# Starting addresses of matmul operands, and the order of a few queue steps, in a clustered-attention kernel with two dense layers

## The chip, the cores and the metric

The kernel runs on 1 core of one Trainium2 chip. The metric is device time in microseconds (us), the median of several executions. Before the change it is 785.4 us (three runs, 784.46 to 785.62).

The engines are named as the profile names them: PE (TensorE, with PEld for its weight loads), DVE (VectorE), ACT (ScalarE), POOL (GpSimd) and SP (SyncE, which here only issues DMAs). "SPq" in a row is the time that SP needs to issue a DMA.

## What is computed

Attention in which a query sees only the keys of its own cluster, and then two dense layers (`moe`, `moe2`) on the 1536 rows that it leaves. B = 2, H = 8, S = 768, D = 64, 16 clusters, 512 columns, 2048 hidden columns, all float32.

```python
q_assign = argmax(normalize(q) @ normalize(centroids).T)      # k_assign likewise
scores = where(q_assign[:, None] == k_assign[None, :], q @ k.T / sqrt(D), -1e9)
x = softmax(scores) @ v                      # -> (B*S, H*D) = (1536, 512)
h = x @ moe_w_in;    x = (h * cos(h)) @ moe_w_out
h = x @ moe2_w_in
g = where(h >= 1, h, where(h <= -1, 0, (h + 1)**2 / 4))
out = g @ moe2_w_out
```

## The kernel before

**Order.** Every engine takes its instructions in the order in which the code issues them (`manual_schedule`). So a step written ahead of another one runs ahead of it on each engine that both use, SP's DMA queue included.

**Attention.** Two heads make a pair; there are 8 pairs (`pairs`). `prep_pair(i)` is a generator of 12 steps, one per `yield`: steps 1 to 4 turn q and k (`ptq`, L492) and split them into a high and a low part `th`, `tl` on POOL (L474, L475); step 5 multiplies with the centroids (`dt`, L513) and moves the result out (`dc`, ACT L516); step 6 turns it back (`pd`, L520); steps 7 to 11 find the cluster as a one-hot row (DVE L529, L530, POOL L532, DVE L537, L539), with `stack_head(0)` in step 9; step 12 turns the one-hots (`po`, `oht`) and calls `one_hots(0)`. `stack_head(h)` is five DMAs from SP that copy `th` and `tl` into the score operands `st` of one head; `one_hots(h)` is four more, from `oht`. Those of head 0 are issued inside the steps. Those of head 1 are appended to the list `second` as one function, `second_head`, and run later. `th` and `tl` have one buffer each; pairs 1, 3 and 5 use a spare slot (`w_1`) in their place, so only pairs 6 and 7 follow one another in the same buffer.

`run_cycle(d, order)` runs one head (d = 0 to 15) from a string of words: S a block of scores (`scores_of`: PE L580 and L583, then DVE L589), E its exponential on ACT (L598), T and t a transpose of p on PE (L635) with its copy out by ACT or DVE (L638), V the product with v (`p_v`, 24 matmuls, L649), R the row sums turned into factors (DVE L605 to L608, POOL L611, a DMA `flat`), B two DMAs that spread the factors (`rb`, L622), X the scaling on DVE (L654), Y the split into `xh`, `xl` on POOL (five instructions, L664 to L669), P the next step of `prep_pair`, K the oldest entry of `second`, W one step of a weight conversion. Even heads use `EVEN`, odd ones `ODD`; d = 0, 13, 14 and 15 have strings of their own. `first_pair()` prepares pair 0 and is written out by hand.

**Dense layers.** `hidden` and `output` are pure matmul streams of 512 columns, fp32r, three matmuls (L785 to L787, `mm3`) for each product. A block is 48 matmuls (four output tiles of 12); there are 24 blocks of `h` and 24 of `y`, 2304 matmuls in all, one stream on PE. In `h` the stationary operand is a weight slot and the moving one `xh` or `xl`. In `y` of the first layer the stationary operand is a weight slot and the moving one `gh` or `gl`; in the second layer these two change places. The weights go round four slots `w_0` to `w_3`: of the eight quarters (l, qi), `h` takes slot 0 where qi is even and slot 2 where it is odd, `y` slot 1 where qi is even and slot 3 where it is odd.

**Layout.** Tiles lie in SBUF one behind the other in the order of the code, each partition's bytes padded to 32. 16384 bytes of scratch and 128 bytes of constants come first. Then `cpool`: ident 512, desc 64, ohscale 32, ohbias 32, own 32, row 96, ones 128, cn32 512, xh 24576, xl 24576. Then `w0pool`: wraw 8192, w_1 16384, wx 4096, w_0 16384. Then `xpool`: rec 128, den 3 x 128, turned 128, line 512, rb 2 x 1536. Then, during attention, `apool` (pt 12 x 1536, nat 6144, css 128, th, tl 6144 each, six st of 6144, dots, oht, four t32 and eq of 1536 each, three v32 of 3072, two mx of 128, eight nm of 32, six p of 3072), and after it, from the same start, `mpool` (w_2, w_3 16384 each, acc 3 x 8192, gh 2 x 8192, gl 2 x 8192 and tiles of 2048).

Lines that the prediction speaks of:

```python
nat[1] = [...]                                                                   # L261
nc.scalar.activation(nat[1][0][...], y.to_broadcast([P, 2]), AF.Exp, scale=0.0)  # L262: loads Exp's table
nc.vector.tensor_scalar(y, y, 1e-30, None, ALU.max)                              # L265: writes y
```

Of the kernel before, what the change touches and what calls it, by code (L numbers as in the profile page):

```python
# [9 lines left out]
F32 = mybir.dt.float32  # L10
# [4 lines left out]
AF = mybir.ActivationFunctionType  # L15
# [4 lines left out]
P = 128  # L20
# [13 lines left out]
def attention_moe_moe(  # L34
# [19 lines left out]
    B, H, S, D = q.shape  # L54
# [20 lines left out]
    cpool = ctx.enter_context(tc.tile_pool(name="cpool", bufs=1))  # L75
    ident = cpool.tile([P, P], F32, name="ident")
    desc = cpool.tile([P, C], F32, name="desc")
# [1 line left out]
    ohbias = cpool.tile([P, 1], F32, name="ohbias")  # L79
    own = cpool.tile([P, 2, 2], F32, name="own")  # L80
    row = cpool.tile([P, 24], I32, name="row")[:, 0:1]
    ones = cpool.tile([P, 32], F32, name="ones")
    mone, half = ones[:, 0:1], ones[:, 1:2]
    cn32 = cpool.tile([P, NPAIR, 2, C], F32, name="cn32")
    nc.gpsimd.iota(row, pattern=[[0, 1]], base=0, channel_multiplier=1)
# [48 lines left out]
    xpool = ctx.enter_context(tc.tile_pool(name="xpool", bufs=1))  # L134
# [70 lines left out]
    with ExitStack() as actx:  # L205
        ap = actx.enter_context(tc.tile_pool(name="apool", bufs=1))
# [47 lines left out]
        def centroid_setup(ct):  # L254
            sq = ct[:, 1]
            nc.vector.tensor_tensor(sq, ct[:, 0], ct[:, 0], ALU.mult)
            ss = ap.tile([P, 32], F32, tag="css", name="css")
            nc.vector.tensor_reduce(ss[:, 0:1], sq, AX.X, ALU.add)
            y = ss[:, 1:2]
            sq = nc.scalar.activation(y, ss[:, 0:1], AF.Sqrt)  # L260
            nat[1] = [w0pool.tile([P, 2, NJ, 2, D], F32, tag="wraw", bufs=1, name="nat1")]  # L261
            nc.scalar.activation(nat[1][0][:, :, 0, 0, 0:1].rearrange("p s o -> p (s o)"),  # L262
                                 y.to_broadcast([P, 2]), AF.Exp, scale=0.0)
            for _ in range(2):
                nc.vector.tensor_scalar(y, y, 1e-30, None, ALU.max)  # L265
                nc.vector.reciprocal(ss[:, 2:3], y)
                nc.vector.scalar_tensor_tensor(
                    ss[:, 3:4], ss[:, 0:1], ss[:, 2:3], y, ALU.mult, ALU.add)
                nc.vector.tensor_scalar(y, ss[:, 3:4], 0.5, None, ALU.mult)
            nc.vector.tensor_scalar(ss[:, 2:3], y, 1e-6, None, ALU.add)  # L270
            nc.vector.reciprocal(ss[:, 3:4], ss[:, 2:3])
            cd = ap.tile([P, HS], F32, tag="pt", bufs=PT_BUFS, name="cd")[:, :P].rearrange(
                "p (r d) -> p r d", r=2)
            for r in range(2):
                done = nc.vector.tensor_scalar(cd[:, r], ct[:, 0], ss[:, 3:4], None, ALU.mult)
            return cd, done

        prepped = {}
        second = []

        def first_pair():
# [35 lines left out]
            def turn(s, hf):  # L317
                qk[s, hf] = bank(f"qk0_{s}_{hf}")
                for jj in range(HJ):
                    nc.tensor.transpose(qk[s, hf][:, jj * P:(jj + 1) * P],  # L320
                                        t[:, s, hf * HJ + jj].rearrange("p h d -> p (h d)"), ident)
# [7 lines left out]
            pc = ps_t.tile([P, HS], F32, tag="t", name="pc")[:, :P]  # L329
            turn(0, 0)  # L330
            turn(0, 1)
            nc.tensor.transpose(pc, cd.rearrange("p r d -> p (r d)"), ident)
            turn(1, 0)
            turn(1, 1)
            run_idle(NIDLE[1])
            pcv = pc.rearrange("p (g h c) -> p g h c", h=2, c=C)
# [3 lines left out]
            for s, hf in ((0, 0), (0, 1), (1, 0)):  # L340
                nc.scalar.activation(t32[s][hf], qk[s, hf], AF.Copy,
                                     scale=D ** -0.5 if s == 0 else 1.0)
# [99 lines left out]
            ps_q.close()  # L442
            ps_s.append(actx.enter_context(tc.tile_pool(name="ps_s", bufs=2, space=PSUM)))
            scores_of(0)
            scores_of(1)
            row_exp(0)
            po = [turn_rows(1, s) for s in range(2)]
            put_rows(1, 0, po[0], nc.scalar)
# [3 lines left out]
        def prep_pair(i):  # L452
# [4 lines left out]
            if i in (1, 3, 5):  # L457
                t2 = w0pool.tile([P, 2, 2, S], F32R, tag="w_1", name=f"t2_{i}")
# [18 lines left out]
            def stack_head(h):  # L477
                rows = slice(h * D, (h + 1) * D)
                t = st[h][0]
                copy(t[0:D], th[rows, 0].unsqueeze(1).to_broadcast([D, 2, S]))  # L480
                copy(t[D:P, 0], tl[rows, 0])
                t = st[h][1]
                copy(t[0:D, 0], th[rows, 1])
                copy(t[D:P, 0], th[rows, 1])
                copy(t[0:D, 1], tl[rows, 1])
# [47 lines left out]
                eq, eq, desc.unsqueeze(1).to_broadcast([P, G, C]), ALU.mult)  # L533
            yield
            stack_head(0)
            yield
            nc.vector.tensor_reduce(mx, eq, AX.X, ALU.max)  # L537
            yield
# [12 lines left out]
            def one_hots(h):  # L551
                for s in range(2):
                    for par in range(2):
                        r0 = par * 64 + s * 32 + h * C
                        dst = st[h][s][D:D + C, 1].rearrange(
                            "c (par jp n) -> c par jp n", par=2, n=P)[:, par]
                        copy(dst, oht[r0:r0 + C])

            def second_head():
                stack_head(1)  # L560
                one_hots(1)

            one_hots(0)
            second.append(second_head)
            yield

        units = [(i, h, hf) for i in range(len(pairs)) for h in range(2) for hf in range(2)]
# [16 lines left out]
                             start=False, stop=True)  # L584

        def row_max(n):
            nm = ap.tile([P, 1], F32, tag="nm", bufs=8, name=f"nm{n}")
            s = ptile[n]
            nc.vector.tensor_reduce(nm, s[:, :, :HS], AX.XY, ALU.max, negate=True)  # L589
            ptile[n] = (s, nm)  # L590

        def row_exp(n):
            s, nm = ptile[n]
            d, jj = divmod(n, NJ)
            if jj == 0:
                dens[d] = xpool.tile([P, 32], F32, tag="den", bufs=3, name=f"den{d}")
            p = ap.tile([P, 2, HS], F32, tag="p", bufs=P_BUFS, name=f"p{n}")
            nc.scalar.activation(p, s[:, :, :HS], AF.Exp, bias=nm,  # L598
                                 accum_out=dens[d][:, jj:jj + 1])
            ptile[n] = p  # L600
# [23 lines left out]
        dens = {}  # L624
# [47 lines left out]


        NDBL = len(units) // 2
        rec = xpool.tile([P, 32], F32, tag="rec", name="rec")
        nc.gpsimd.memset(rec, 0.0)
        made = chain.from_iterable(prep_pair(i) for i in range(1, len(pairs)))

# [2 lines left out]
        def scores_of(n):  # L681
            scores(n, 0)
            scores(n, 1)
            row_max(n)

        def run_cycle(d, order):


            for word in order.split():
                what, arg = word[0], int(word[1:] or 0)  # L690
                n = NJ * d + arg
                if what == "S":
                    if n < NJ * NDBL:
                        scores_of(n)
                elif what == "E":
                    if n < NJ * NDBL:
                        row_exp(n)
                elif what in "Tt":
                    p_transpose(2 * d + arg // NJ, arg % NJ, what == "t")
                    next_slot()  # L700
                elif what == "P":
                    next(made, None)
                elif what == "R":
                    inverse(d)
                elif what == "V":
                    p_v(d)
                elif what == "X":
                    if opsum:
                        x_rows(min(opsum))
                elif what == "K":  # L710
                    if second:
                        second.pop(0)()
                elif what == "B":
                    spread()
                elif what == "Y":
                    if x32s:
                        x_parts()
                elif what in "Ww":
                    pump(1 if d >= FIRST + (what == "w") else 0)
                elif what == "N":  # L720
                    next_slot()
            if d == 3:
                issue_chunk(0)

        PRE = "P S8 P E8"
        BEGIN = "S3 P T0 T1 S4 E3 P T2 E4 P T3 S5 E5 t4 T5 S6 T6 T7 E6 P R S7 t8 T9 E7 T10 P S8 P E8 B P S9 P t11 S10 V E9 E10"
        EVEN = "P S5 T0 T1 P t2 E5 S6 T3 P T4 E6 t5 S7 R T6 P T7 E7 S8 X T8 T9 E8 Y t10 B S9 P w P E9 t11 S10 W E10 V"
        ODD = "K S5 T0 T1 P t2 S6 E5 T3 X T4 t5 S7 Y E6 P T6 R E7 T7 S8 P E8 t8 T9 S9 T10 B P t11 E9 W S10 V P P E10 W"
        LATE_ODD = "S5 T0 T1 t2 E5 S6 T3 K R T4 t5 S7 X Y E6 T6 T7 E7 S8 E8 t8 T9 S9 T10 B t11 S10 E9 V W W W E10"
        LATE_EVEN = "S5 T0 t1 t2 E5 S6 T3 T4 E6 R T5 S7 X Y E7 T6 S8 T7 t8 W S9 E8 t9 B T10 E9 t11 W S10 V E10 W"  # L730
        LAST = "S5 T0 E5 t1 T2 T3 X t4 R t5 Y t6 T7 t8 B T9 t10 T11 W V W W W X Y"
        first_pair()
        for d in range(-1, NDBL):
            run_cycle(d, PRE if d < 0 else BEGIN if d == 0 else
                      {13: LATE_ODD, 14: LATE_EVEN, 15: LAST}.get(d, (EVEN, ODD)[d % 2]))
        manual.close()
# [138 lines left out]
```

## Time and profile before

| | us |
|---|---|
| median of the runs shown | 785.4 (784.46, 785.40, 785.62) |
| the profiled execution, its own time | 787.31 |
| its span, first to last instruction | 785.5 |
| PE busy in the span | 770.9 (98%) |
| DVE, ACT, POOL busy | 569.5, 361.3, 254.9 |
| mean granted TensorE clock | 0.993 of full |

The profile was taken on one execution. A row of a timeline gives the start, the duration, the engine, the line, the operation with its tiles (out<-in) and, in brackets, how long the engine had been idle before and what ended that. Matmuls overlap, so the duration of one says little; the distance between two starts says what each costs. A `x6` row merges six in a row. TensorE's clock has two levels here, 2.4 GHz (1.00) and 1.2 GHz (0.50).

### The profile page before, as it was taken

The page shows a single profiled execution, that of the slowest core. Times are in us where ns is not written, and L with a number is a line of the kernel's source. Part 1 is how long each engine was busy: PE and PEld are TensorE (multiplying, and loading weights), DVE is VectorE, ACT ScalarE, POOL GpSimd, SP SyncE. Part 2 cuts the span into 40 slices and gives each one's busy share as a digit, 9 for nine tenths or more (in the row PEclk, how much of TensorE's full clock was granted, in tenths as well). Part 3 has the DMA queues.
Part 4 walks back from the last instruction along what each step waited for, and adds up shares of the span by engine and source line. Part 5 has one row for each costly group of instructions (what it writes and reads, how often), then busy time and mean ns, then how long its engine had stood idle before and what let it go on. Part 6 is the DMA issues. An engine that isn't in the chain of part 4 may idle for free.

```text
span 785.5 us, 10592 instructions
## 1 busy us (share of the span) xinstructions
PE 770.9 (98%) x3885; PEld 609.9 (78%) x3886; DVE 569.5 (73%) x824; ACT 361.3 (46%) x671; POOL 254.9 (32%) x390
## 2 busy tenths in 40 slices
PE   8899999999899999999999999999999999999998
PEld 4677777776676888888888888888888888888886
DVE  5767688797688778687788887888867787555552
ACT  4867677777574644534334342333434232212220
POOL 5447449465534522222222123422312121111110
PEclk9999999999899999999999999999999999999999
DMA  8874676665342122213131122021121111000012
GB/s 193 215 160 120 181 156 183 155 174 123 86 130 75 54 108 75 86 55 108 53 101 62 54 78 83 3 104 55 54 101 61 53 54 55 0 1 1 27 41 93
DMA packets 49523, 70.10 MB, mean 89 GB/s; under 512 B 28576, under 2 KB 33664, under 8 KB 49472
## 3 DMA queue, kind: packets, MB, share of 16 engines
q1 hardware_dynamic: 49328, 69.40, 31.5%
q8 instruction: 30, 0.49, 0.3%
q14 instruction: 21, 0.17, 0.1%
q10 hardware_dynamic: 144, 0.03, 0.0%
HBM read 46.17 MB, written 3.19 MB: 63 GB/s over the span
## 4 chain that ended last, share of the span: by engine, by line
PE 89%; ACT 4%; DVE 3%; DMA 2%; issue 1%; SPq 0%; POOL 0%; ACTq 0%; DVEq 0%
PE h L785 11%; PE h L787 11%; PE y L787 11%; PE h L786 11%; PE y L786 11%; PE y L785 11%; PE o L649 7%; PE pt L635 5%; PE s L580 4%; PE s L583 3%; ACT p L598 2%; ACT p_t L640 1%; DVE nm L589 1%; PE ptq L492 1%; DMA wraw<-in_moe_w_in_dram 1%
## 5 line engine op out<-in xcount | busy, mean ns | idle before, releaser
L747 POOL TENSOR_SCALAR gh<-g 128x512 fp32r<-128x512 f32 x96 | 71.4, 744 | 294.5 <-DVE g L778 161.0
L785 PE MATMUL h<-xh,w 128*128 128x512 f32 x384 | 150.6, 392 | 0.2 <-ACT p L598 0.2
L787 PE MATMUL h<-xh,w 128*128 128x512 f32 x384 | 150.7, 393 | 0.0
L786 PE MATMUL h<-xl,w 128*128 128x512 f32 x384 | 150.6, 392 | 0.0
L589 DVE TENSOR_REDUCE nm<-s 128x1 f32<-128x768 f32 x96 | 91.3, 952 | 45.4 <-PE s L583 43.7
L598 ACT ACTIVATE p<-s,nm 128x768 f32<-128x768 f32 x96 | 87.2, 909 | 23.6 <-DVE nm L589 20.2
L774 ACT ACTIVATE p<-h,ones 128x512 f32<-128x512 f32 x48 | 33.1, 690 | 136.7 <-DVE m L773 136.3
L751 DVE TENSOR_TENSOR gl<-g,gh 128x512 fp32r<-128x512 f32 x96 | 72.1, 751 | 21.5 <-POOL gh L747 16.0
L635 PE MATMUL pt<-ident,p 128*128 128x128 f32 x576 | 82.2, 278 | 3.4 <-DVE p_t L638 2.9
L787 PEld LDWEIGHTS h<-xh,w 128*128 128x128 f32 x384 | 72.1, 188 | 16.6 <-issue 0.6
L785 PEld LDWEIGHTS h<-xh,w 128*128 128x128 f32 x384 | 72.1, 188 | 16.4 <-issue 0.4
L786 PEld LDWEIGHTS h<-xl,w 128*128 128x128 f32 x384 | 72.2, 188 | 16.1
L635 PEld LDWEIGHTS pt<-ident,p 128*128 128x128 f32 x576 | 68.6, 143 | 12.1 <-ACT p L598 4.0
L640 ACT ACTIVATE p_t<-pt 128x384 f32<-128x384 f32 x126 | 57.8, 491 | 43.2 <-PE pt L635 42.3
L580 PE MATMUL s<-st,st 128*128 128x384 f32 x192 | 74.6, 388 | 1.6 <-ACT p L598 1.0
L787 PE MATMUL y<-gh,w 128*128 128x512 f32 x192 | 75.3, 392 | 0.0
L786 PE MATMUL y<-gl,w 128*128 128x512 f32 x192 | 75.3, 392 | 0.0
L785 PE MATMUL y<-gh,w 128*128 128x512 f32 x192 | 75.3, 392 | 0.0
L785 PE MATMUL y<-w,gh 128*128 128x512 f32 x192 | 75.3, 392 | 0.0
L787 PE MATMUL y<-w,gl 128*128 128x512 f32 x192 | 75.2, 392 | 0.0
L786 PE MATMUL y<-w,gh 128*128 128x512 f32 x192 | 75.2, 392 | 0.0
L824 DVE TENSOR_TENSOR acc<-y,acc 128x512 f32<-128x512 f32 x72 | 49.2, 685 | 35.6 <-PE y L787 35.6
(120 smaller groups left out, 1310.7 us busy)
## 6 DMA issues: line engine op xcount, KB each, us to landing
wraw<-in_moe_w_in_dram SPq DMA_DIRECT2D x16, 1024.0 KB
wraw<-in_moe_w_out_dram SPq DMA_DIRECT2D x16, 1024.0 KB, 4.7
st<-t SPq DMA_DIRECT2D x24, 192.0 KB, 4.3
st<-th SPq DMA_DIRECT2D x10, 384.0 KB, 3.8
st<-th SPq DMA_DIRECT2D x20, 192.0 KB, 3.9
st<-tl SPq DMA_DIRECT2D x19, 192.0 KB
nat<-in_q_dram SPq DMA_DIRECT2D x8, 384.0 KB, 4.1
nat<-in_k_dram SPq DMA_DIRECT2D x8, 384.0 KB, 4.8
```

The lines of the kernel that those rows point to most:

```text
L580: nc.tensor.matmul(s[:, step, :HS], qt[:, 0, cols], kt[:, 0, kc], start=True, stop=False)
L589: nc.vector.tensor_reduce(nm, s[:, :, :HS], AX.XY, ALU.max, negate=True)
L598: nc.scalar.activation(p, s[:, :, :HS], AF.Exp, bias=nm, accum_out=dens[d][:, jj:jj + 1])
L635: nc.tensor.transpose(ps[:, jj * P:(jj + 1) * P], p[:, kt * P:(kt + 1) * P], ident)
L640: nc.scalar.activation(pt, ps, AF.Copy)
L649: nc.tensor.matmul(o[hf * D:(hf + 1) * D], prepped[i][0][:, h, kt], pts.pop((2 * d + hf, kt)), start=kt == 0, stop=kt == NJ - 1)
L747: nc.gpsimd.tensor_scalar(hi, g, 1.0, 0.0, ALU.mult, ALU.add)
L751: nc.vector.tensor_tensor(lo, g, hi.bitcast(F32), ALU.subtract)
L785: nc.tensor.matmul(o, lh, rh, start=first, stop=False)
L786: nc.tensor.matmul(o, lh, rl, start=False, stop=False)
L787: nc.tensor.matmul(o, ll, rh, start=False, stop=last)
L824: nc.vector.tensor_tensor(a, po, a, ALU.add)
```

## The change

It does five things.

1. Tile sizes: `ones` grows by 512 bytes, `den` goes from 3 x 128 to 4 x 32, `rec` from 128 to 256 bytes and lends its second half to the centroid factors, whose own tile (`css`) goes, and `nm` has seven buffers in place of eight.
2. Exp's table is loaded by an instruction that reads `desc` in place of `y`.
3. In `first_pair` the third group of transposes stands ahead of the centroids' transpose `pc`, and steps 5 and 6 of pair 1 stand behind the first two score blocks (they were the two P of `PRE`).
4. `second_head` is split: `stack_head(1)` and `one_hots(1)` are two entries of `second`, and K stands twice in `BEGIN` and `EVEN` (before S8 and before S9) in place of once at the head of `ODD` and in `LATE_ODD`. In `BEGIN` B moves ahead of S8.
5. In `ODD`, X moves from behind T3 to before S8 and Y from behind S7 to behind S8. In `LATE_EVEN` a W moves ahead of V.

```diff
     row = cpool.tile([P, 24], I32, name="row")[:, 0:1]
-    ones = cpool.tile([P, 32], F32, name="ones")
+    ones = cpool.tile([P, 160], F32, name="ones")
     mone, half = ones[:, 0:1], ones[:, 1:2]
...
             nc.vector.tensor_tensor(sq, ct[:, 0], ct[:, 0], ALU.mult)
-            ss = ap.tile([P, 32], F32, tag="css", name="css")
+            ss = spare
             nc.vector.tensor_reduce(ss[:, 0:1], sq, AX.X, ALU.add)
...
             nc.scalar.activation(nat[1][0][:, :, 0, 0, 0:1].rearrange("p s o -> p (s o)"),
-                                 y.to_broadcast([P, 2]), AF.Exp, scale=0.0)
+                                 desc[:, 0:2], AF.Exp, scale=0.0)
             for _ in range(2):
...
             turn(0, 1)
+            turn(1, 0)
             nc.tensor.transpose(pc, cd.rearrange("p r d -> p (r d)"), ident)
-            turn(1, 0)
             turn(1, 1)
...
             scores_of(0)
+            next(made)
             scores_of(1)
+            next(made)
             row_exp(0)
...
             stack_head(0)
+            second.append(stack_head)
             yield
...
-            def second_head():
-                stack_head(1)
-                one_hots(1)
-
             one_hots(0)
-            second.append(second_head)
+            second.append(one_hots)
             yield
...
         def row_max(n):
-            nm = ap.tile([P, 1], F32, tag="nm", bufs=8, name=f"nm{n}")
+            nm = ap.tile([P, 1], F32, tag="nm", bufs=7, name=f"nm{n}")
             s = ptile[n]
...
             if jj == 0:
-                dens[d] = xpool.tile([P, 32], F32, tag="den", bufs=3, name=f"den{d}")
+                dens[d] = xpool.tile([P, 8], F32, tag="den", bufs=4, name=f"den{d}")
             p = ap.tile([P, 2, HS], F32, tag="p", bufs=P_BUFS, name=f"p{n}")
...
         NDBL = len(units) // 2
-        rec = xpool.tile([P, 32], F32, tag="rec", name="rec")
+        pair_of = xpool.tile([P, 64], F32, tag="rec", name="rec")
+        rec, spare = pair_of[:, :32], pair_of[:, 32:]
         nc.gpsimd.memset(rec, 0.0)
...
                     if second:
-                        second.pop(0)()
+                        second.pop(0)(1)
                 elif what == "B":
...
-        PRE = "P S8 P E8"
-        BEGIN = "S3 P T0 T1 S4 E3 P T2 E4 P T3 S5 E5 t4 T5 S6 T6 T7 E6 P R S7 t8 T9 E7 T10 P S8 P E8 B P S9 P t11 S10 V E9 E10"
-        EVEN = "P S5 T0 T1 P t2 E5 S6 T3 P T4 E6 t5 S7 R T6 P T7 E7 S8 X T8 T9 E8 Y t10 B S9 P w P E9 t11 S10 W E10 V"
-        ODD = "K S5 T0 T1 P t2 S6 E5 T3 X T4 t5 S7 Y E6 P T6 R E7 T7 S8 P E8 t8 T9 S9 T10 B P t11 E9 W S10 V P P E10 W"
-        LATE_ODD = "S5 T0 T1 t2 E5 S6 T3 K R T4 t5 S7 X Y E6 T6 T7 E7 S8 E8 t8 T9 S9 T10 B t11 S10 E9 V W W W E10"
-        LATE_EVEN = "S5 T0 t1 t2 E5 S6 T3 T4 E6 R T5 S7 X Y E7 T6 S8 T7 t8 W S9 E8 t9 B T10 E9 t11 W S10 V E10 W"
+        PRE = "S8 E8"
+        BEGIN = "S3 P T0 T1 S4 E3 P T2 E4 P T3 S5 E5 t4 T5 S6 T6 T7 E6 P R S7 t8 T9 E7 T10 P B S8 P E8 P K S9 K P t11 S10 V E9 E10"
+        EVEN = "P S5 T0 T1 P t2 E5 S6 T3 P T4 E6 t5 S7 R T6 P T7 E7 K S8 X T8 T9 E8 Y t10 B K S9 P w P E9 t11 S10 W E10 V"
+        ODD = "S5 T0 T1 P t2 S6 E5 T3 T4 t5 S7 E6 P T6 R E7 T7 X S8 Y P E8 t8 T9 S9 T10 B P t11 E9 W S10 V P P E10 W"
+        LATE_ODD = "S5 T0 T1 t2 E5 S6 T3 R T4 t5 S7 X Y E6 T6 T7 E7 S8 E8 t8 T9 S9 T10 B t11 S10 E9 V W W W E10"
+        LATE_EVEN = "S5 T0 t1 t2 E5 S6 T3 T4 E6 R T5 S7 X Y E7 T6 S8 T7 t8 W S9 E8 t9 B T10 E9 t11 W S10 W V E10"
         LAST = "S5 T0 E5 t1 T2 T3 X t4 R t5 Y t6 T7 t8 B T9 t10 T11 W V W W W X Y"
```

## Rows read from the trace of the kernel before

**Rows 1.** Busy time by stretch: us, PE, PEld, DVE, ACT, POOL, PEclk, DMA, GB/s

```profile
24.00:197.00 173.00, 171.33 (x1171) 128.63 (x1169) 129.09 (x206) 126.73 (x284) 96.83 (x152) 1.00 0.66 159
197.00:212.00 15.00, 11.90 (x65) 10.88 (x65) 8.69 (x15) 8.42 (x18) 7.13 (x16) 0.77 0.43 97
...
246.00:782.00 536.00, 535.68 (x2346) 435.88 (x2344) 388.42 (x519) 191.09 (x296) 124.17 (x150) 1.00 0.18 60
...
20.00:24.00 4.00, 2.26 (x17) 1.86 (x14) 2.38 (x4) 3.53 (x9) 2.65 (x4) 1.00 1.02 279
```

**Rows 2.** Timeline of PE, first layer: first and last matmul of four blocks of 48

```profile
273.60 0.40 PE L785 MATMUL y<-gh,w 128*128 128x512 f32 x1
...
284.56 0.39 PE L787 MATMUL y<-gh,w 128*128 128x512 f32 x1
284.79 0.39 PE L785 MATMUL h<-xh,w 128*128 128x512 f32 x1
...
295.46 0.39 PE L787 MATMUL h<-xh,w 128*128 128x512 f32 x1
...
306.88 0.40 PE L785 MATMUL h<-xh,w 128*128 128x512 f32 x1
...
317.85 0.39 PE L787 MATMUL h<-xh,w 128*128 128x512 f32 x1
...
340.47 0.39 PE L785 MATMUL y<-gh,w 128*128 128x512 f32 x1
...
351.14 0.39 PE L787 MATMUL y<-gh,w 128*128 128x512 f32 x1
```

**Rows 3.** The same of one block of the second layer

```profile
538.64 0.40 PE L785 MATMUL y<-w,gh 128*128 128x512 f32 x1
...
549.57 0.40 PE L787 MATMUL y<-w,gl 128*128 128x512 f32 x1
```

**Rows 4.** Timeline of all engines around 200 us, and of SP ahead of it

```profile
180.70 1.12 SPq L622 DMA_DIRECT2D rb<-flat  x2
181.87 0.67 SPq L470 DMA_DIRECT2D st<-th  x1
...
186.35 3.06 SPq L470 DMA_DIRECT2D st<-oht  x4
...
188.51 0.21 DVE L608 STREAM_TRANSPOSE turned<-rec 128x32 f32<-128x32 f32 x1
...
188.75 0.51 POOL L474 TENSOR_SCALAR th<-t 128x384 fp32r<-128x384 f32 x1 [7.98 <-DMA st<-th]
...
201.83 0.55 DVE L537 TENSOR_REDUCE mx<-eq 128x24 f32<-128x384 f32 x1 [3.22 <-POOL eq L532]
...
202.90 0.90 PE L635 MATMUL pt<-ident,p 128*128 128x128 f32 x3 [2.93 <-DVE p_t L638]
```

**Rows 5.** Chain that ended last: starts of V in heads 9 to 12

```profile
164.40 4.02 PE o L649 x24
...
178.15 4.02 PE o L649 x24
...
192.68 4.02 PE o L649 x24
...
211.92 4.02 PE o L649 x24
```

**Rows 6.** DMA issues: KB each, median us from issue to landing

```profile
rb<-flat SPq DMA_DIRECT2D x32, 96.0 KB, 2.7
```

**Rows 7.** Timeline of all engines in the first 23 us

```profile
4.69 0.15 DVE L265 TENSOR_SCALAR css<-css 128x1 f32<-128x1 f32 x1 [1.78 <-ACT nat L262]
...
7.61 0.36 PE L332 MATMUL pc<-ident,cd 128*128 128x128 f32 x1 [1.38 <-DVE cd L275]
...
7.77 1.48 PE L320 MATMUL qk<-ident,nat 128*128 128x128 f32 x6
...
22.76 0.55 PE L520 MATMUL pd<-ident,dc 128*128 128x128 f32 x3 [1.41 <-ACT dc L516]
```

## The prediction

> **What bounds the kernel now.** I read the busy times by stretch first. In the dense layers PE is busy for 535.7 of 536 us, and in the attention stage from 24 to 197 us for 171.3 of 173, at the full clock; DVE, the next, has 129 and 388 us there [rows 1]. So two thirds of the time are one stream of matmuls in which nothing waits, and what such a stretch is worth is the distance between two starts, not a wait. The second view is therefore PE's timeline in the dense layers. The reader is to divide: a block has 48 matmuls, so 47 distances. The `h` block from 284.79 takes 10.67 us (227.0 ns each), that from 306.88 takes 10.97 (233.4); the `y` block from 273.60 takes 10.96 (233.2), that from 340.47 takes 10.67 (227.0) [rows 2]. All have 512 columns and the same clock. The third view is the stretch with lost time, 197 to 212 us: PE busy 11.9 of 15, clock 0.77 [rows 1]. The fourth is the start, where PE waits for others.
>
> **Which blocks are slow.** The working is in the sizes of the layout. Ahead of `xh` lie 16384 + 128 + 512 + 64 + 3 x 32 + 96 + 128 + 512 = 17920 bytes, which is 1536 past a multiple of 2048; `xl`, `w_1` and `w_0` follow at whole multiples and stand at 1536 too. `xpool` starts at 112128 and takes 128 + 384 + 128 + 512 + 3072 = 4224, so `w_2`, `w_3`, `gh` and `gl` stand at 1664. Now the blocks: `h` from slot 0 has 1536 against 1536 and is quick; `h` from slot 2 has 1664 against 1536 and is slow; `y` from slot 1 has 1536 against 1664, slow; `y` from slot 3 has 1664 against 1664, quick [rows 2]. In the second layer, where weights and `g` change places, `y` from slot 1 takes 10.93 us, 232.6 each [rows 3]. The reading that fits: a matmul costs 6 ns more where its stationary and its moving operand start 128 bytes apart modulo 512 (steps of f and e are multiples of 512 and change nothing inside a block). It isn't the crossing of a multiple of 2048 as such, since every quick block crosses one.
>
> **The change, part by part.**
>
> *Addresses.* `ones` moves `xh` to 18432 = 9 x 2048, and `xl`, `w_1`, `w_0` with it. `xpool` then starts at 112640 and takes 256 + 128 + 128 + 512 + 3072 = 4096, so `mpool` and `apool` start at 116736 = 57 x 2048: `w_2`, `w_3`, `gh`, `gl` at 0, and, with `css` gone, `th`, `tl` and `st` too. All dense blocks become equal in offset. The slow ones are the `y` of even and the `h` of odd quarters, 12 blocks in each layer: 12 x 48 x (233.3 - 227.0) = 3.6 us and 12 x 48 x (232.6 - 227.0) = 3.2 us, together 6.8. All of it is on the path, since PE doesn't wait there; DVE would be busy for 388 of 529 us, with room. Both operands of a score come from `st` tiles that stood at one offset before, so I take nothing for them; the bounds are 0 and the same 6.3 ns on 384 matmuls, 2.4 us. The other tiles move as well. `p` starts 1792 past a multiple before and 2016 after, which is no longer a multiple of 128; no row has an operand so placed. Bounds for its 576 transposes are 0 and the 6.3 ns of the dense blocks, 3.6 us; I take 0, because their stationary `p` and their moving `ident` differ by 128 modulo 512 already, and the nearest case in kind is their own present one.
>
> The Trainium skill speaks against this part. "SBUF — State Buffer", section Who interferes with whom, gives PE two read ports, one for the moving operand and one for weight loads, and says that PE never waits on anyone; by that the 6.8 us would not be there, and the sum would be 6.0. The rows differ by block in a stretch without waits, which the page doesn't explain, so I go by the rows and keep the page's case as a rival.
>
> *Head-1 stacking.* Around 200 us the chain is: POOL may not write `th` of pair 7 until the stacking DMAs of pair 6 have read it, and stands for 7.98 us until 188.75; its work then runs late up to L532, DVE waits 3.22 us for that with the copies of `p_t` behind it, and PE waits 2.93 us until 202.90 [rows 4]. From V to V, head 12 takes 19.24 us, head 10, a normal even one, 13.75 [rows 5]: 5.5 lost, 2.9 in the wait and 2.6 in matmuls at half clock behind it. What does the change do to it? K's five DMAs now stand ahead of the two `rb` of their head. SP issues these one behind the other, `rb` at 180.70 and the five at 181.87 [rows 4], so they move by 1.2 us only, because SP is the bound there, not the place in the code. POOL's step of pair 7 and all behind it come 1.2 us sooner (X and Y change their places among POOL's steps, not its sum ahead of L532), and PE's wait becomes 1.7. Whether 1.7 us still brings the clock down is open: after the wait of 1.41 us at 22.76 [rows 7] the clock in that stretch was 1.00 [rows 1], after 2.93 it fell. I take no fall: 1.2 + 2.6 = 3.8 us. Bounds: 1.2 (the clock falls as before) and 5.5 (the wait goes).
>
> On SP K now passes the two `rb` of its head and the loads and weight chunks of the steps behind it. The loads aren't waited for soon. The two `rb` come later by the five issues, 186.35 - 181.87 = 4.5 us. In head 10 they would be issued by 181.82 + 4.5 = 186.3 and land 2.7 later [rows 6], at 189.0. X, now before S8, comes behind L608, which ended at 188.72 [rows 4]. So X may wait 0.3 us where it waited for nothing; S8's L589 is queued behind it on DVE and ACT's exponential behind that. Score blocks have two buffers, which cover that much. I take 0. POOL has Y later and nearer to L532, but is busy for 96.8 of 173 us only [rows 1], so I take 0; the bound is a wait like the 2.93 us in each odd head, which is the second rival in another queue. W ahead of V puts one DVE or ACT instruction behind the last copy that V needs: nothing. The fourth `den` and the seventh `nm` loosen and tighten what never waited: nothing.
>
> *The start.* DVE waits 1.78 us at 4.69 for an Exp instruction that only loads a table [rows 7]; with `desc` as operand some 1.5 of it go, and the centroids' chain ends that much sooner. PE waited 1.38 us for it at 7.61 [rows 7], but now the third group of transposes stands ahead, and when its k arrives no row shows (between q's arrival and 7.77). So `pc` gains between 0 and 1.4; I take 0.8. Of the six transposes that followed it, 1.48 us long [rows 7], three are now done before: 0.7. Steps 5 and 6 behind the first scores put `dc` ahead of two exponentials on ACT and fill PE's wait of 1.41 us at 22.76 [rows 7]: between 0 and 1.4, I take 0.7, as the second exponential then bounds. Sum 2.2, bounds 0.7 and 3.5. Later stages are bound by PE, so it stays.
>
> **Sum.** 6.8 + 3.8 + 2.2 = 12.8 us. The profiled execution's own 787.3 (span 785.5 and 1.8 around it) becomes 774.5; it lies 1.9 over the median of the runs, so the median 785.4 becomes 772.6. With all bounds but the first term's: 785.4 - 6.8 - 5.5 - 3.5 - 2.4 = 767.2, and 785.4 - 6.8 - 1.2 - 0.7 + 3.6 = 780.3.
>
> **Rivals.**
> 1. The offsets are innocent and slots 1 and 2 are slow for another reason, which stays. For: only four slots speak. Against: the order holds where the roles are swapped. 785.4 - 6.0 = 779.4.
> 2. Slower: the stacking DMAs ahead of `rb` hold X in the five even heads 2 to 10, in SP's queue and then DVE's. Each wait of the size at 202.90 costs 5.5 us with the clock: 772.6 + 27.5 = 800. It turns the sign from 2.6 us per head; my reckoning has 0.3. For: the margin is thin. Against: two score buffers lie between.
> 3. `p`'s new start costs the full 3.6 us: 776.2.
> 4. With both operands at 0 the matmuls lose their whole surplus over 512 columns at 2.4 GHz, 213.3 ns: 2304 x 13.7 = 31.6 us more, 741. Against: 1536 is a multiple of 512 as 0 is, and the quick `h` blocks have both operands there.
>
> **How the numbers follow.** The forecast has 0.74, rival 1 0.11, rival 2 0.08, rival 3 0.05, rival 4 0.02. The range from 768 to 780 holds the forecast's bounds nearly whole, rival 1 and rival 3. About 0.2% (1.6 us) is what a measurement of this kernel can tell from no change: faster by more 0.92 (all but rival 2), within it 0.03 (rival 2 with some 2.6 us per head), slower 0.05 (rival 2 with more).
>
> **What would show it.** Right: all dense blocks take 10.67 us; head 12 takes some 15 us from V to V at full clock; the first scores start 1.5 us sooner. Wrong: blocks of 10.9 us remain (term 1), a POOL wait of 8 us remains with a PE wait near 200 us and clock 0.5 (term 2), X waits for a DMA in odd heads (rival 2), transposes of p further apart than now (rival 3).

## The result and the profile after

The changed kernel takes 773.07 us (median of four runs, 772.34 to 774.09), the kernel before 785.35 (784.46 to 785.62) beside it: ratio 0.9846, 95% interval 0.9829 to 0.9864. Forecast were 772.6, in a range from 768 to 780. The profiled execution of after took 772.82, span 771.0; that of before had 787.31, span 785.5. So the traces lie 14.5 us apart and the medians 12.3; where the other 2 us belong is a question below.

| stretch of the trace, us | before | after | difference |
|---|---|---|---|
| start of the span to the first V | 36.05 | 33.40 | -2.65 |
| first V to last V (15 heads) | 212.77 | 208.37 | -4.40 |
| first to last dense matmul | 536.10 | 528.67 | -7.44 |

First the busy time of after by stretch (us, PE, PEld, DVE, ACT, POOL, granted clock, DMA, GB/s), which answers to [rows 1]; its lines stand a little lower or higher than those of before (copies of `p_t` L637, V L648, X L653).

```profile
24.00:197.00 173.00, 171.46 (x1172) 128.71 (x1173) 127.82 (x204) 125.88 (x283) 100.08 (x160) 1.00 0.66 161
197.00:212.00 15.00, 14.00 (x94) 10.34 (x92) 13.25 (x20) 9.78 (x24) 6.25 (x11) 1.00 0.63 136
...
246.00:782.00 536.00, 521.20 (x2299) 431.39 (x2298) 384.30 (x512) 187.71 (x292) 118.77 (x141) 1.00 0.17 59
```

The reader is to see the second line: PE busy 14.0 of 15 us at full clock, where before had 11.9 at 0.77. In the third, the stretch now holds the end of the span, so PE's time there is its work, not its share. What a matmul costs is in PE's timeline of after, the same `y`, `h` and second-layer `y` blocks as in [rows 2, 3] that were slow:

```profile
266.56 0.39 PE L785 MATMUL y<-gh,w 128*128 128x512 f32 x1
...
277.21 0.39 PE L787 MATMUL y<-gh,w 128*128 128x512 f32 x1
...
299.20 0.39 PE L785 MATMUL h<-xh,w 128*128 128x512 f32 x1
...
309.85 0.39 PE L787 MATMUL h<-xh,w 128*128 128x512 f32 x1
...
527.68 0.39 PE L785 MATMUL y<-w,gh 128*128 128x512 f32 x1
...
538.33 0.39 PE L787 MATMUL y<-w,gl 128*128 128x512 f32 x1
```

Each is 10.65 us for 47 distances, 226.7 ns (the mean of all but the first block), where they took 10.96, 10.97 and 10.93. And the place of the stall, all engines (answers to [rows 4, 5]):

```profile
175.19 0.54 PE L648 MATMUL o<-p_t,v 128*64 128x384 f32 x2
...
176.78 0.67 SPq L472 DMA_DIRECT2D st<-th  x1
...
178.15 2.12 SPq L472 DMA_DIRECT2D st<-th  x2
...
181.24 1.83 SPq L621 DMA_DIRECT2D rb<-flat  x2
...
183.65 0.51 POOL L476 TENSOR_SCALAR th<-t 128x384 fp32r<-128x384 f32 x1 [5.78 <-ACT p_t L639]
...
190.21 0.54 PE L648 MATMUL o<-p_t,v 128*64 128x384 f32 x2
...
197.04 0.55 DVE L540 TENSOR_REDUCE mx<-eq 128x24 f32<-128x384 f32 x1 [0.84 <-POOL eq L534]
...
198.11 0.55 PE L634 MATMUL pt<-ident,p 128*128 128x128 f32 x3 [0.56 <-DVE p_t L637]
...
204.81 0.54 PE L648 MATMUL o<-p_t,v 128*64 128x384 f32 x2
```

The `rb` now stand behind the stacking DMAs. POOL's write of `th` comes 8.46 us behind the V of head 10 (before 10.67; the timeline has that V at 178.08, the chain of [rows 5] 0.07 later), DVE waits 0.84 us for POOL (3.22), PE 0.56 (2.93), and head 12 takes 204.81 - 190.21 = 14.60 us (19.24). POOL still waits 5.78 us. The row names a copy of ACT, but the write starts 3.38 us behind the end of the last two `th` issues (178.15 + 2.12 = 180.27). It started 3.37 us behind them in before, and 3.30 to 3.36 in the three runs below that put K, X and Y back. So it is most likely still these DMAs that POOL waits for.

### The profile page after: what moved, and what is told of

Its sections match the earlier page's. It is cut to its first block, busy times and chain, and to the rows that moved or that the text cites. A ratio compares the mean times of both kernels' runs of the same rounds, so it can differ in the third digit from the quotient of the medians.

```text
span 771.0 us, 10599 instructions
## 1 busy us (share of the span) xinstructions
PE 760.2 (99%) x3885; PEld 606.4 (79%) x3886; DVE 570.3 (74%) x824; ACT 360.0 (47%) x671; POOL 254.3 (33%) x390
## 4 chain that ended last, share of the span: by engine, by line
PE 83%; ACT 4%; DMA 4%; DVE 2%; POOL 2%; SPq 2%; issue 1%; ACTq 0%; POOLq 0%; DVEq 0%
PE h L785 11%; PE h L787 11%; PE h L786 11%; PE y L786 11%; PE y L787 11%; PE y L785 11%; PE o L648 5%; PE pt L634 3%; PE s L579 3%; ACT p L597 2%; PE s L582 2%; DMA st<-t 1%; ACT p_t L639 1%; DMA flat<-line 1%; SPq L472 1%
## 5 line engine op out<-in xcount | busy, mean ns | idle before, releaser
L751 DVE TENSOR_TENSOR gl<-g,gh 128x512 fp32r<-128x512 f32 x96 | 73.7, 768 | 22.3 <-POOL gh L747 16.1
L786 PEld LDWEIGHTS h<-xl,w 128*128 128x128 f32 x384 | 72.1, 188 | 14.9
L154 ACT ACTIVATE wx<-wraw 128x1024 f32<-128x1024 f32 x32 | 36.5, 1142 | 85.8 <-DVE w L173 33.9
L634 PEld LDWEIGHTS pt<-ident,p 128*128 128x128 f32 x576 | 66.9, 141 | 11.4 <-ACT p L597 5.2
```

Source lines behind the costliest of these rows:

```text
L154: nc.scalar.activation(x, high.bitcast(F32), AF.Abs)
L634: nc.tensor.transpose(ps[:, jj * P:(jj + 1) * P], p[:, kt * P:(kt + 1) * P], ident)
L751: nc.vector.tensor_tensor(lo, g, hi.bitcast(F32), ALU.subtract)
L786: nc.tensor.matmul(o, lh, rl, start=False, stop=False)
```

## Experiments

The kernel before had 786.6, 786.2 and 786.4 us beside the experiments, which ran in three sets, and 785.4 beside the result. Where one microsecond matters I therefore compare each kernel's ratio to the kernel before beside it, times 785.4 us. Heads are counted as in the prediction: head n lasts from the V of d = n - 1 to that of d = n; the "even heads 2 to 10" of its second rival are the heads 3 to 11 in this count.

### Term 1: the addresses

**Sizes alone.** The kernel before with the sizes of `ones`, `den`, `rec`, `nm` and `css` of the change, and nothing else.

```diff
-    ones = cpool.tile([P, 32], F32, name="ones")
+    ones = cpool.tile([P, 160], F32, name="ones")
...
-            ss = ap.tile([P, 32], F32, tag="css", name="css")
+            ss = spare
```

> The kernel before with the new tile sizes alone (term 1): order and operands of the steps as before. Theory of the offsets: every dense block takes 10.65 to 10.67 us (226.7 ns from start to start), the first to the last dense matmul 7.4 us less than before, and the stall near 200 us stays, with PE waiting about 2.9 us for DVE and the clock at half behind it; time 785.4 - 6.8 to 7.5 = about 778.2. Rival (the slow slots have another reason, which the other edits took away): blocks of 10.9 us remain, time about 785.

Measured: 778.18 us, ratio 0.9908 (0.9879 to 0.9937), so 7.2 us. All blocks take 10.65 us but the first, into which the end of the attention falls (17.3 us in every kernel), and the first to the last dense matmul 528.66 us, as after. The `y` block that was slow:

```profile
270.73 0.39 PE L786 MATMUL y<-gh,w 128*128 128x512 f32 x1
...
281.38 0.39 PE L788 MATMUL y<-gh,w 128*128 128x512 f32 x1
```

PE's wait near 200 us stays (3.08), and from the first V to the last 211.85 us pass, 0.92 less than before; the clock is at half for a shorter time behind that wait (the columns of [rows 1], where before had 0.77):

```profile
197.00:212.00 15.00, 11.58 (x68) 8.82 (x68) 10.68 (x17) 8.40 (x19) 7.80 (x15) 0.89 0.43 100
```

So the sizes bring the dense layers' gain, alone and whole.

**The two sides 128 bytes apart again.** The kernel after; `xh`, `xl`, `w_0`, `w_1` move down, `rec` grows by as much, so that all behind stands where it did.

```diff
-    ones = cpool.tile([P, 160], F32, name="ones")
+    ones = cpool.tile([P, 128], F32, name="ones")
...
-        pair_of = xpool.tile([P, 64], F32, tag="rec", name="rec")
+        pair_of = xpool.tile([P, 96], F32, tag="rec", name="rec")
```

> The kernel after, with xh, w_0 and w_1 moved to 128 bytes below a multiple of 2048, all else where it is; so the two sides stand 128 bytes apart again. Theory of the offsets: the same 12 blocks in each layer are slow again (233 ns), the others 226.7; 773.1 + 6.6 to 7.4 = about 780. A theory that a start off a multiple of 2048 is what costs: all blocks that use xh, w_0 or w_1 are slower, on whichever side, so also the h of slot 0, which were quick before. Rival that the slots have another reason: 773.

Measured: 780.87 us, ratio 0.9928 (0.9914 to 0.9943): 6.4 us of the gain are gone. PE's timeline, the first two blocks of [rows 2], `y` from slot 1 and `h` from slot 0:

```profile
267.27 0.40 PE L785 MATMUL y<-gh,w 128*128 128x512 f32 x1
...
278.23 0.39 PE L787 MATMUL y<-gh,w 128*128 128x512 f32 x1
278.46 0.39 PE L785 MATMUL h<-xh,w 128*128 128x512 f32 x1
...
289.13 0.39 PE L787 MATMUL h<-xh,w 128*128 128x512 f32 x1
```

10.96 and 10.67 us, the same two numbers as in [rows 2], block for block, though `xh` stands at 1920 past a multiple now and not at 1536. In the `h` block both operands start at 1920, and it is quick; so a start off a multiple of 2048 isn't what costs.

**All at 1536.** The kernel after with `ones` as before, so that every large operand stands 1536 past a multiple of 2048.

```diff
-    ones = cpool.tile([P, 160], F32, name="ones")
+    ones = cpool.tile([P, 32], F32, name="ones")
```

> The kernel after, with every large operand at 1536 past a multiple of 2048, where xh, w_0 and w_1 stood before: equal on both sides, but no multiple of 2048. Theory of the equal offsets: every block quick, 226.7 ns, time 773.1, the same as the kernel after. Theory that multiples of 2048 are what is needed, as the change has it: the blocks lose what the change gained, 233 ns in half or all of them, 780 to 788.

Measured: 773.5 us, ratio 0.9843 (0.9818 to 0.9868), the same as after; blocks of 10.65 us (267.25 to 277.90 for the `y` of slot 1). What the change names, multiples of 2048, isn't needed; that both sides start alike is.

**Other distances.** As with 128 bytes, but 512, 256, 64 and 32 (in `ones` 160 - bytes / 4, in `rec` 64 + bytes / 4).

> The kernel after, with xh, w_0 and w_1 moved to 512 bytes below a multiple of 2048. My reading (what counts is the distance modulo 512): every block quick, 226.7 ns, time about 773. A reading modulo 2048: the 24 mixed blocks slow, 233 ns, about 780.

> The kernel after, with xh, w_0 and w_1 moved to 256 bytes below a multiple of 2048. Any distance that is no multiple of 512 costs the same: 233 ns in 24 blocks, time 780. The cost grows with the distance: about 239 ns, time 787. The modulus is 256 rather than 512: 226.7, time 773. I lean to the first.

> The kernel after, with xh, w_0 and w_1 moved to 64 bytes below a multiple of 2048. Two readings, both open: the cost comes with any distance that is no multiple of 512 (the 12 + 12 blocks at 232.5 to 233, as at 128 bytes; time 780), or it grows with the distance and is about half at 64 bytes (230, time 776), or 64 bytes are within one unit and cost nothing (226.7, time 773). I lean to the first.

> The kernel after, with xh, w_0 and w_1 moved to 32 bytes below a multiple of 2048. 64 and 128 bytes of distance cost 6 ns in a block, 256 and 512 nothing. If every distance that is no multiple of 256 costs: 780 to 781. If less than 64 bytes is within one unit of the memory: 773.

The times at 32, 64, 256 and 512 bytes are of one run each. The mean distance between two starts in PE's timeline, by layer and kind, over the `y` of odd and `h` of even quarters ("like": both operands from one side) and the other 24 blocks ("unlike"), without the very first block:

| distance, bytes | like, ns | unlike, ns | first to last dense matmul, us | time, us |
|---|---|---|---|---|
| 0 (after) | 226.7 | 226.7 | 528.67 | 773.07 |
| 32 | 227.0 to 227.3 | 233.3 | 536.91 | 781.29 |
| 64 | 227.0 to 227.4 | 230.6 to 233.3 | 536.15 | 780.66 |
| 128 | 226.9 to 227.0 | 232.4 to 233.2 | 536.11 | 780.87 |
| 256 | 226.7 | 226.7 | 528.67 | 773.72 |
| 512 | 226.7 | 226.7 | 528.69 | 774.06 |

The `h` block that is the third of [rows 2], at 32 and then at 256 bytes (two kernels):

```profile
300.12 0.40 PE L785 MATMUL h<-xh,w 128*128 128x512 f32 x1
...
311.08 0.40 PE L787 MATMUL h<-xh,w 128*128 128x512 f32 x1
```

```profile
299.94 0.39 PE L785 MATMUL h<-xh,w 128*128 128x512 f32 x1
...
310.60 0.39 PE L787 MATMUL h<-xh,w 128*128 128x512 f32 x1
```

10.96 against 10.66. So the cost is nearly a step: some 6.6 ns for the tried distances below 256, nothing at 256 and 512. I had leaned to a cost at 256; that was wrong. "Modulo 512" in the prediction fails there, and "modulo 256" fits all that was tried. It isn't shown beyond that: no distance such as 384, above 256 and no multiple of it, was tried, and it would tell a modulus of 256 from a cost that comes only where two starts differ by less than 256 modulo some larger number.

At 64 bytes the step isn't clean. The 230.6 is a mean of two sorts: of the six unlike `y` blocks of the first layer the four with a like block ahead of them take 10.77 or 10.78 us (229.3 ns), and the two with an unlike one ahead 10.97 (233.3). The first and the third of them:

```profile
266.92 0.40 PE L785 MATMUL y<-gh,w 128*128 128x512 f32 x1
...
277.70 0.39 PE L787 MATMUL y<-gh,w 128*128 128x512 f32 x1
...
311.06 0.40 PE L785 MATMUL y<-gh,w 128*128 128x512 f32 x1
...
322.02 0.39 PE L787 MATMUL y<-gh,w 128*128 128x512 f32 x1
```

### Term 2: the stacking and its neighbours

**K alone back.** The kernel after, with the DMAs of head 1 (both K) at the start of the odd heads, as before (in `BEGIN` and `LATE_ODD` as in these two).

```diff
-        EVEN = "P S5 T0 T1 P t2 E5 S6 T3 P T4 E6 t5 S7 R T6 P T7 E7 K S8 X T8 T9 E8 Y t10 B K S9 P w P E9 t11 S10 W E10 V"
-        ODD = "S5 T0 T1 P t2 S6 E5 T3 T4 t5 S7 E6 P T6 R E7 T7 X S8 Y P E8 t8 T9 S9 T10 B P t11 E9 W S10 V P P E10 W"
+        EVEN = "P S5 T0 T1 P t2 E5 S6 T3 P T4 E6 t5 S7 R T6 P T7 E7 S8 X T8 T9 E8 Y t10 B S9 P w P E9 t11 S10 W E10 V"
+        ODD = "K K S5 T0 T1 P t2 S6 E5 T3 T4 t5 S7 E6 P T6 R E7 T7 X S8 Y P E8 t8 T9 S9 T10 B P t11 E9 W S10 V P P E10 W"
```

> The kernel after, with the five head-1 stacking DMAs and their register reads back at the start of the odd heads, behind both rb (term 2 undone; X, Y and the other edits stay). My theory: POOL again stands about 8 us for the write of th of pair 7, PE waits 1.7 to 3 us for it near 195 us, the clock falls to half behind it, V to V of head 12 is 18.5 to 19.2 us; time 773.1 + 3.9 to 4.6 = 777 to 778. Rival (the stall went because X and Y are later): no stall, time about 773.

Measured: 775.68 us, ratio 0.9856 (0.9841 to 0.9871): 2.6 us by the medians, 0.8 by the ratio, whose interval overlaps with that of after. So the times alone don't show the cost; the trace does. Its timeline near 200 us (all engines):

```profile
178.82 0.67 SPq L472 DMA_DIRECT2D st<-th  x1
...
185.79 0.51 POOL L476 TENSOR_SCALAR th<-t 128x384 fp32r<-128x384 f32 x1 [7.23 <-ACT t L500]
...
190.44 0.54 PE L648 MATMUL o<-p_t,v 128*64 128x384 f32 x2
...
200.02 0.55 PE L634 MATMUL pt<-ident,p 128*128 128x128 f32 x3 [2.23 <-DVE p_t L637]
...
207.66 0.54 PE L648 MATMUL o<-p_t,v 128*64 128x384 f32 x2
```

The stall is back: POOL waits 7.23 us, PE 2.23, head 12 takes 17.22 us, and the granted clock of 198 to 206 us is 0.79. With the 0.6 us that head 8 loses again, from the first V to the last 211.43 us pass, 3.06 more than after. The time is less than I expected; for K's place alone ratio and traces leave 0.8 to 3.1 us.

**X and Y alone back.** K stays early.

```diff
-        ODD = "S5 T0 T1 P t2 S6 E5 T3 T4 t5 S7 E6 P T6 R E7 T7 X S8 Y P E8 t8 T9 S9 T10 B P t11 E9 W S10 V P P E10 W"
+        ODD = "S5 T0 T1 P t2 S6 E5 T3 X T4 t5 S7 Y E6 P T6 R E7 T7 S8 P E8 t8 T9 S9 T10 B P t11 E9 W S10 V P P E10 W"
```

> The kernel after, with X and Y of the odd heads back at their old places, ahead of S7 and E6; K stays early. The margin of the second rival: the two rb now stand behind the five stacking DMAs in SP's queue, and X would come 5 to 6 us sooner than they land; if that holds DVE long enough, PE waits 2 us or more in each of the five odd heads 3 to 11, with the clock behind it: 773.1 + 10 to 27 = 783 to 800. If the two score buffers cover it: 773 to 774, with the small losses of heads 6 and 10 (0.4 and 0.5 us) changed.

Measured: 781.42 us, ratio 0.9934 (0.9915 to 0.9953): 6.9 us of the gain gone by the ratio, 8.3 by the medians. DVE's waits, 24 to 246 us (total, times, longest), and the timeline of one:

```profile
DVE rb L653 <- DMA rb<-flat: 9.7, 6, 2.9
```

```profile
187.50 1.86 SPq L621 DMA_DIRECT2D rb<-flat  x2
...
191.56 0.56 DVE L653 TENSOR_TENSOR rb<-o,rb 128x384 f32<-128x384 f32 x1 [2.93 <-DMA rb<-flat]
```

The longest wait of PE, from its own timeline:

```profile
194.96 0.55 PE L634 MATMUL pt<-ident,p 128*128 128x128 f32 x3 [1.78 <-ACT p_t L639]
```

X waits six times, and heads 3, 5, 7, 9 and 11 take 15.87, 16.20, 15.85, 15.88 and 17.52 us where after has 14.55, 14.54, 14.93, 14.55 and 15.02. This is the second rival's mechanism, in the place that it named. Its price was too high: 0.9 to 2.5 us per head and not 5.5, since PE's own waits stay at 1.8 us and below, and the granted clock is 1.00 from 61 to 205 us.

**Both back.** K, X, Y and W as before; sizes and start of after, and the B of `BEGIN` too.

> The kernel after with the orders of the attention stage as before (K, X, Y and W), the sizes and the start kept: both parts of term 2 undone together. If the two belong together and are worth what heads 10 to 12 lost in the traces: 773.1 + 4.2 to 4.6 = 777.5. If K alone is what the place of the stacking is worth: 775.7, as with K alone undone. If the effects of the two single undoings added up (2.6 and 8.3): 784.

Measured: 776.45 us, ratio 0.9878 (0.9861 to 0.9896): 2.5 us by the ratio, 3.4 by the medians, 3.2 from the first V to the last. POOL's and PE's wait (3.12 us) are those of before, and head 12 takes 18.09 us (18.45 with the sizes alone):

```profile
POOL th L476 <- DMA st<-th: 8.3, 1, 8.3
```

The singles don't add up. A part of that may stand on SP, ahead of K: the four issues from `oht` there, in before and in after.

```profile
176.79 3.58 SPq L470 DMA_DIRECT2D st<-oht  x4
```

```profile
174.22 2.46 SPq L472 DMA_DIRECT2D st<-oht  x4
```

In the fourteen profiled executions they take 3.48 to 3.87 us in the five with X and Y early (before twice, the sizes alone, X and Y back, both back), and 2.46 to 2.59 in eight with X and Y late, K back among them. A ninth, with the start undone (below), has 3.35, so the place of X and Y isn't all of it; how it would reach SP wasn't tried. From the kernel with both back, X and Y later change next to nothing (775.7 with K late), K earlier costs 5 us (781.4), and both together gain 3.4 (773.1). The move of X and Y is worth what it spares K.

### Term 3 and the profile's own chance

**The start's edits undone.**

```diff
-                                 desc[:, 0:2], AF.Exp, scale=0.0)
+                                 y.to_broadcast([P, 2]), AF.Exp, scale=0.0)
...
-            turn(1, 0)
             nc.tensor.transpose(pc, cd.rearrange("p r d -> p (r d)"), ident)
+            turn(1, 0)
...
-            next(made)
             scores_of(1)
-            next(made)
...
-        PRE = "S8 E8"
+        PRE = "P S8 P E8"
```

> The kernel after with the three edits of the start undone: the table-loading Exp reads y again, the third group of transposes stands behind pc, steps 5 and 6 run ahead of the first scores. My prediction had 2.2 us for them: 773.1 + 2.2 = 775.3. A theory formed from the run of the sizes alone, whose first V started at 34.1 us without these edits, against 33.2 to 34.3 in the seven kernels that have them: the edits are worth about 0.4 us, and most of the 2.65 us that the profiled execution of before was later is its own clock fall at 7.8 us, which came by chance with a late arrival of q: 773.3 to 773.8.

Measured: 775.78 us, ratio 0.9877 (0.9857 to 0.9897): 2.7 us by the medians, 2.4 by the ratio, nearer to the prediction than to the newer theory, though the intervals of the two ratios overlap a little. The trace gives less at the start. Its first V starts at 35.27 us, 1.9 behind that of after, with a stretch at half clock from 20.85 us on, behind PE's wait of 1.43 us for `dc`; its heads 11 and 12 are 1.2 us longer than in after, though nothing is changed there. The clock's fall isn't the whole difference: three of the six executions had a mean clock of 1.00 and took 775.22 to 775.49 us, three of after at 1.00 took 772.34 to 773.32. But these are two sets, and the kernel before was 1.0 us slower beside the first.

**The kernel before, a second profiled execution.** Nothing is edited.

> The kernel before once more, for a second profiled execution of its start and of head 12. If the clock fall at 7.8 us was chance: first scores at 14.5 to 15.3 us, first V at 34 to 35 us, no stretch at half clock ahead of 12 us. If it belongs to the kernel: first scores at about 16.5, first V at 36. Head 12 takes 18.4 to 19.3 us from V to V either way.

Measured: 785.62 us, span 783.8. PE's timeline of this execution, and then of after:

```profile
7.56 0.33 PE L332 MATMUL pc<-ident,cd 128*128 128x128 f32 x1 [1.32 <-DVE cd L275]
...
14.80 0.42 PE L580 MATMUL s<-st,st 128*128 128x384 f32 x1
...
21.07 0.55 PE L520 MATMUL pd<-ident,dc 128*128 128x128 f32 x3 [1.43 <-ACT dc L516]
```

```profile
6.56 0.27 PE L333 MATMUL pc<-ident,cd 128*128 128x128 f32 x1
...
14.60 0.41 PE L579 MATMUL s<-st,st 128*128 128x384 f32 x1 [0.70 <-DVE st L424]
...
19.97 0.45 PE L579 MATMUL s<-st,st 128*128 128x384 f32 x1 [1.04 <-ACT p L597]
```

The first V starts at 34.36 us here, 1.7 sooner than in the execution that the prediction read; there the clock was at half for some 3.4 us from 7.8 us on, here it isn't, though PE waits as long for `pc`. So that fall was this execution's and not the kernel's. Head 12 takes 19.25 us again. Against this execution, after is shorter by 1.0 us at the start, 4.4 in the attention and 7.4 in the dense layers, 12.8 together, near the medians' 12.3: 1.7 of the 2 us that were left over are the chance of the first profile.

## Where the prediction was right and wrong

- **Term 1, 6.8 us: right, a little small.** 7.4 in the trace, 7.2 and 6.4 in the two runs that do or undo it alone. The quick blocks gained too, 10.662 to 10.653 us: behind an unlike block the first distances of a quick one were slow (231 to 232 ns, three of them in the `h` block from 284.79), so that the reading of 227.0 ns for them was itself 0.3 too high. The mechanism stands, with 256 in the place of 512 as far as distances were tried. `p` at 2016 past a multiple costs nothing (its transposes start 109.3 ns apart, before 109.5), and neither do the scores (178 ns both times). Neither tests the rule, since by the sizes of the layout `p` and `ident` stood 128 apart modulo 256 before and 96 in after, and the scores' operands alike in both. V does, and it shows a limit: its `v` and `p_t` stood 128 apart modulo 256 before and alike in after, and its 24 matmuls take 3.605 us from the first start to the last both times. So the cost is shown for the fp32r matmuls of 512 columns; V's f32 matmuls, with 64 columns of weights, don't have it. The Trainium skill, "SBUF — State Buffer", section Who interferes with whom, gives PE two independent read ports, for the moving operand and for weight loads. By that alone the distance between the two starts would change nothing; 226.7 against 233.3 ns at otherwise equal work decides, and the start addresses count. Which part of the memory does it, no run shows.
- **Term 2, 3.8 us: near in sum, with two sizes off.** "They move by 1.2 us only, because SP is the bound there" is the step that was too small: K's first DMA stands 1.59 us behind the V of head 10 in after, 3.79 before, so 2.2 us sooner. With K back it stands at 2.94, so 1.35 belong to K. The other 0.85 lie ahead of it on SP, where the four issues from `oht` took 2.46 us and not 3.58. The prediction took that stretch as fixed; by the runs it goes with the place of X and Y in all executions but one (under "Both back"). PE's wait became 0.56 instead of 1.7, so this run doesn't answer whether 1.7 us bring the clock down. The other runs do, for this place: 1.57 us (256 bytes apart, at 198.84) and 1.78 (X and Y back, at 194.96) did not, 2.23 did (K back). So the choice of no fall agrees with what they show. Head 12 gained 4.6 us, head 8 0.6 (PE's wait of 0.39 us for ACT's `t` is gone); heads 7 and 11, where the prediction took 0, lost 0.4 and 0.5. In head 7 the trace has a wait of 0.17 us for a copy of `p_t`, and the rest isn't explained; it takes 14.9 us in every kernel with X and Y late. Head 11 takes 14.55 to 15.21 us in the seven kernels with the order and the start of after, so its loss comes and goes. Some of the 4.4 us isn't the order's: 197 to 212 us had a mean clock of 0.77 before [rows 1], 15 x 0.23 x 2 = 6.9 us at half, and 0.89, 3.3 us, with the sizes alone, behind nearly the same wait (2.93 and 3.08 us). Whether the sizes shorten the fall or chance does isn't settled; both executions of before had the long one, the three kernels with the new sizes and the stall the short one. So the order itself is worth the 2.5 to 3.4 of the run with both back, below the 3.8 that was taken for it.
- **X's margin: right.** X waits for nothing in after; POOL's Y neither. The run with X and Y back shows that this was the place to watch.
- **Term 3, 2.2 us: within its bounds, the path in part wrong.** `pc` came 1.0 us sooner than in that second execution (I took 0.8) and the wait for `dc` is gone, for two others of 1.04 and 0.51 us on ACT's `p`. But "the first scores start 1.5 us sooner" failed: they start at 14.60, against 16.49 us in the execution that the prediction read but 14.80 in the second one, because they now wait 0.70 us for DVE's `st`. What the start gains comes behind them. The bounds of 0.7 and 3.5 hold all that was measured: 1.3 us between the mean first V of the ten kernels with the edits (33.6) and of the four executions without (34.9), 2.4 and 2.7 in the timed run. What lies between the two isn't settled.
- **The basis.** The sum was made against the profiled execution and carried to the median by 1.9 us, as if the surplus were spread over all parts. Of it 1.7 us were in one place, the start. Term 3 was partly read from that stretch [rows 7]: the 1.48 us of six transposes at half clock are 0.82 in the second execution. That the sum came within 0.5 us is in part luck: term 1 (6.8) measured 6.4 to 7.4, the order (3.8) 2.5 to 3.4 with the rest of the attention's gain open, and the start (2.2) 1.0 to 2.7, so misses of either sign could cancel.
- **Rivals.** 1 (offsets innocent, 779.4) falls with the runs at 128 bytes and of the sizes alone. 2 (X held, 800) didn't come to pass, but is real. 3 (776.2) and 4 (741) fall by the spacing in after: 109.3 and 226.7 ns.

## What to carry to other kernels

In a stream of matmuls that waits for nothing, compare the distance between starts block by block; where equal work has two speeds, write down the start addresses of both operands, and pad so that they agree (here modulo 256 bytes, 3% of the slow blocks). Measure one block after it: V's matmuls gained nothing from the same step. When DMAs are pulled ahead in a queue, what they overtake comes late: move its reader as well, or the gain turns into a loss (5 us here, where both moves together gain 3.4). Look at a second execution before a stall at the start is put into a sum.

## What the runs showed of the hardware

- A 512-column fp32r matmul starts every 226.7 ns on the mean of a block where its stationary and moving operand start alike or 256 or 512 bytes apart, and every 232.4 to 233.4 ns, by layer and kind, where they start 32, 64 or 128 bytes apart; only four `y` blocks of the first layer at 64 took 229.3, and why is open. The slow pace carries over into the first distances of the quick block behind.
- The clock doesn't follow from the length of a wait alone: 1.4 us of PE's waiting near 21 us stood ahead of a fall to 1.2 GHz in the run with the start undone, and of none in either execution of before; of the ten kernels with the start's edits, which all wait 1.05 and 0.5 us near 20 us, the clock fell behind these waits in one (512 bytes apart); a wait of 3.1 us near 200 us was followed by 3.4 us at half clock with the sizes alone and by 6.8 in the second execution of before.
- SP needed 2.46 to 3.87 us for the same four DMA issues from `oht` in fourteen executions, the longer times where X and Y stand early and once with the start undone; what holds it wasn't tried.
